# A gated linear recurrence with a multiplicative FFN: from half-sequences with a scan tree to 512-token chunks in a written order

## The chip, the cores and the metric

The kernel runs on one core of a Trainium2 chip. The metric is the device time of one launch in microseconds (us). The core has TensorE (PE; its weight loads are shown apart as PEld), VectorE (DVE), ScalarE (ACT), GpSimd (POOL) and SyncE (SP), each with its own instruction queue, worked off in order, and 16 DMA engines that all queues share. PE reads SBUF and writes PSUM.

## The reference

Inputs x, r_gate and i_gate are 4 sequences x 5824 tokens x 256 channels; the result is 23296 tokens x 256. Types are float32.

```python
a_base = sigmoid(a_param)
log_a = 8.0 * sigmoid(r_gate) * np.log(np.clip(a_base, 1e-06, 1 - 1e-06))
a_t = np.exp(log_a)
norm = np.sqrt(np.maximum(1.0 - a_t * a_t, 1e-06))
x_gated = norm * sigmoid(i_gate) * x
for t in range(S):                       # per sequence and channel, h = 0 at its start
    h = a_t[:, t] * h + x_gated[:, t]
    y[:, t] = h
out = ((y @ w1) * (y @ w2)) @ w3 @ w_out   # w1, w2: 256x1024, w3: 1024x1024, w_out: 1024x256
```

Both kernels use that the last two products are linear: w3 @ w_out is formed once on the chip as a 1024x256 weight (`wp_sb`), so the FFN has an "up" part (two products 256 -> 1024, multiplied elementwise) and a "down" part (1024 -> 256).

## The kernel before

Channels lie on partitions (two blocks of 128, `NCB`), time along the free axis. The outer loops run over 4 sequences and 2 halves of 2912 tokens (`HSEG`, `T`). A half goes through four steps.

1. Gates (lines 160-207): for each group of up to 512 tokens, POOL issues the loads of r, i and x, cast to bf16 by the DMA; PE transposes each into PSUM; ACT takes the sigmoid of r into `a_big` (L190) and of i into `sig_i` (L199); DVE multiplies `sig_i` with the transposed x into `b_big` (L206).
2. Over the whole half (L210-L214): ACT's Exp gives the decay `a_big`, Square and Sqrt give the norm in `t_big`, and DVE multiplies it into `b_big`.
3. The scan, all on DVE: a tree over blocks of 8, 4, 7 and 13 (`LEVELS`). In each block of 8, seven steps of three instructions over every eighth element (L223-L225), then `rec_scan` on the block ends (L122-L147), then the carry goes back into the blocks (L250-L255), which write `y_bf`. `hprev` hands the state from the first half to the second.
4. FFN: for each group of 512 tokens, 8 steps m of `pa` (L265) and `pb` (L270), ACT copies `pa` to `sa` (L275), DVE makes `gt` = `sa` x `pb` (L277); then 32 matmuls `pout` (L290), copied to `ot` (L299) by ACT and DVE in turn and stored over SP's queue.

Ahead of the loops, w3 is loaded whole, transposed on PE and multiplied with w_out (L85-L102). The order on each engine comes from the framework's scheduler, which orders instructions by dependence and priority, within what the buffers allow: `bigpool` and `ybuf` have two buffers each, so the gates of the next half may run beside the scan or FFN of this one. PSUM has 4 banks for `pa`/`pb`, 2 for the transposes and 2 for `pout`.

Of the kernel before, what the change touches and what calls it, by code (L numbers as in the profile page):

```python
# [10 lines left out]
AF = mybir.ActivationFunctionType  # L12


@with_exitstack
def kernel(
# [14 lines left out]

# [16 lines left out]
    NG = (T + GT - 1) // GT

    consts = ctx.enter_context(tc.tile_pool(name="consts", bufs=1))  # L50
    wpool = ctx.enter_context(tc.tile_pool(name="wpool", bufs=1))
    psum = ctx.enter_context(tc.tile_pool(name="psum", bufs=4, space=bass.MemoryType.PSUM))
    psum_t = ctx.enter_context(tc.tile_pool(name="psum_t", bufs=2, space=bass.MemoryType.PSUM))
    psum_o = ctx.enter_context(tc.tile_pool(name="psum_o", bufs=2, space=bass.MemoryType.PSUM))

    ident = consts.tile([P, P], F32, tag="ident")
    make_identity(nc, ident)
    ident_bf = consts.tile([P, P], BF16, tag="ident_bf")
    make_identity(nc, ident_bf)

    log_a8 = consts.tile([P, NCB], F32, tag="log_a8")
    nc.sync.dma_start(out=log_a8, in_=a_param.rearrange("(cb p) -> p cb", p=P))
    nc.scalar.activation(out=log_a8, in_=log_a8, func=AF.Sigmoid)
    nc.scalar.activation(out=log_a8, in_=log_a8, func=AF.Ln)
    nc.scalar.mul(out=log_a8, in_=log_a8, mul=8.0)

    w1_sb = wpool.tile([P, NCB, DFF], BF16, tag="w1")
    nc.gpsimd.dma_start(out=w1_sb, in_=moe_w1.rearrange("(cb p) f -> p cb f", p=P))
    w2_sb = wpool.tile([P, NCB, DFF], BF16, tag="w2")
    nc.gpsimd.dma_start(out=w2_sb, in_=moe_w2.rearrange("(cb p) f -> p cb f", p=P))  # L70
    wp_sb = wpool.tile([P, KD, D], BF16, tag="wp")

    with tc.tile_pool(name="wtemp", bufs=1) as wtemp:
        w3_sb = wtemp.tile([P, KD, DFF], F32, tag="w3")
        nc.sync.dma_start(out=w3_sb, in_=moe_w3.rearrange("(ko p) f -> p ko f", p=P))
        wo_sb = wtemp.tile([P, KD, D], BF16, tag="wo")
        nc.gpsimd.dma_start(out=wo_sb, in_=moe_w_out.rearrange("(ko p) f -> p ko f", p=P))

        w3T_sb = wtemp.tile([P, KD, DFF], BF16, tag="w3T")
        for jo in range(KD):  # L80
            for ii4 in range(2):
                pt = psum_t.tile([P, 4, P], F32, name="pt", tag="ptr")
                for ii in range(4):
                    i_in = ii4 * 4 + ii
                    nc.tensor.matmul(  # L85
                        out=pt[:, ii, :],
                        lhsT=w3_sb[:, i_in, jo * P:(jo + 1) * P],
                        rhs=ident, is_transpose=True,
                        start=(ii == 0), stop=(ii == 3))
                nc.scalar.copy(  # L90
                    out=w3T_sb[:, jo, ii4 * 4 * P:(ii4 * 4 + 4) * P],
                    in_=pt.rearrange("p a b -> p (a b)"))

        for mi in range(KD):
            po = psum_t.tile([P, D], F32, name="po", tag="ptr")
            for k in range(KD):
                nc.tensor.matmul(
                    out=po,
                    lhsT=w3T_sb[:, k, mi * P:(mi + 1) * P],
                    rhs=wo_sb[:, k, :],  # L100
                    start=(k == 0), stop=(k == KD - 1))
            nc.scalar.copy(out=wp_sb[:, mi, :], in_=po)  # L102

    bigpool = ctx.enter_context(tc.tile_pool(name="bigpool", bufs=2))
    ybuf = ctx.enter_context(tc.tile_pool(name="ybuf", bufs=2))
    carry = ctx.enter_context(tc.tile_pool(name="carry", bufs=2))
    inpool = ctx.enter_context(tc.tile_pool(name="inpool", bufs=1))
    tmp_pool = ctx.enter_context(tc.tile_pool(name="tmp", bufs=3))
    small = ctx.enter_context(tc.tile_pool(name="small", bufs=1))
    gpool = ctx.enter_context(tc.tile_pool(name="gpool", bufs=8))  # L110
    opool = ctx.enter_context(tc.tile_pool(name="opool", bufs=2))

    def rec_scan(a, b, levels, top=False):
# [228 lines left out]
```

## Time and profile before

| | |
|---|---|
| device time, three runs | 1126.17, 1127.95, 1128.27 us (median 1127.95) |
| profiled execution, span from first to last instruction | 1126.3 us |
| PE / PEld busy | 677.1 us (60%) / 412.9 us (37%) |
| DVE busy | 830.8 us (74%) |
| ACT busy | 553.8 us (49%) |
| POOL busy | 122.7 us (11%) |
| mean granted TensorE clock | 0.774 of full speed |
| DMA | 66.19 MB, mean 59 GB/s |

No time of the profiled execution apart from its span is recorded; the span lies within the range of the three runs, and 1.65 us under their median. Shares are means over stages of different kinds, so a stage has to be read by itself. The slices of the page divide the span into 40 equal parts of 28.2 us; a digit is the busy share in tenths. PE's ends are modelled and its matmuls overlap, so its progress is read better from the starts of successive matmuls than from its busy time.

### The profile page before, as it was taken

How to read it: one execution, taken by the hardware profiler on the slowest of the kernel's cores; microseconds unless marked ns; L12 is line 12 of the kernel's file. 1: busy time of each engine (PE TensorE's matmuls, PEld its weight loads, DVE VectorE, ACT ScalarE, POOL GpSimd, SP SyncE). 2: the span in 40 equal slices, each digit the busy share in tenths (PEclk: the TensorE clock that was granted, in tenths of full speed). 3: DMA queues.
4: the chain of work that ended last, by engine and by line, in shares of the span. 5: the costliest groups of instructions: out<-in, count | busy, mean ns of one | idle time of the engine just before them, and what ended most of it. 6: DMA issues, size and time to landing. Idle time of an engine off the chain costs nothing.

```text
span 1126.3 us, 12072 instructions
## 1 busy us (share of the span) xinstructions
PE 677.1 (60%) x4197; PEld 412.9 (37%) x4240; DVE 830.8 (74%) x1308; ACT 553.8 (49%) x733; POOL 122.7 (11%) x179
## 2 busy tenths in 40 slices
PE   2733238849952317884993332885896141689498
PEld 2522214435541213452562221443554121245155
DVE  0118999995533999998551799999663399999855
ACT  2584563424467284342558447342455828234144
POOL 2222200000021210001002221000002120000000
PEclk9755559988975558996995555998898555799699
DMA  9576521122164642113117552211316360001011
GB/s 252 76 93 75 68 29 45 38 46 62 39 107 54 77 56 38 38 39 50 57 52 102 65 69 28 55 38 42 56 48 107 45 87 0 19 33 43 13 57 51
DMA packets 100365, 66.19 MB, mean 59 GB/s; under 512 B 4560, under 2 KB 98768, under 8 KB 100304
## 3 DMA queue, kind: packets, MB, share of 16 engines
q0 software_dynamic: 74160, 37.37, 26.2%
q1 hardware_dynamic: 26144, 28.06, 7.3%
q8 instruction: 33, 0.54, 0.2%
q14 instruction: 28, 0.23, 0.1%
HBM read 78.91 MB, written 23.86 MB: 91 GB/s over the span
## 4 chain that ended last, share of the span: by engine, by line
issue 45%; DVE 23%; PE 16%; ACT 8%; DMA 4%; POOL 3%; POOLq 0%; DVEq 0%
PE pb L270 5%; PE pa L265 5%; PE pout L290 5%; DVE isc L223 4%; DVE gt L277 3%; DVE b_big L224 3%; DMA x_t<-in_x_dram 2%; DVE b_big L206 2%; DVE t_big L250 2%; ACT a_big L210 2%; DVE y_bf L252 2%; ACT t_big L213 2%; ACT t_big L212 2%; DMA r_t<-in_r_gate_dram 2%; DVE b_big L123 1%
## 5 line engine op out<-in xcount | busy, mean ns | idle before, releaser
L275 ACT CAST sa<-pa 128x512 bf16<-128x512 f32 (+1 forms) x384 | 216.4, 564 | 271.8 <-PE pa L265 107.8
L277 DVE TENSOR_TENSOR gt<-sa,pb 128x512 bf16<-128x512 bf16 (+1 forms) x384 | 248.0, 660 | 44.4 <-ACT sa L275 30.4
L265 PE MATMUL pa<-y_bf,w_sb 128*128 128x512 bf16 (+1 forms) x740 | 223.2, 380 | 82.4 <-DVE y_bf L252 58.2
L270 PE MATMUL pb<-y_bf,w_sb 128*128 128x512 bf16 (+1 forms) x753 | 226.8, 381 | 11.5 <-DVE gt L277 8.0
L290 PE MATMUL pout<-wp_sb,gt 128*128 128x256 bf16 (+1 forms) x1472 | 187.5, 273 | 5.4 <-DVE gt L277 4.0
L187 PE MATMUL pr<-ident_bf,r_t 128*128 128x128 bf16 (+1 forms) x368 | 50.2, 281 | 183.8 <-ACT sig_i L199 108.6
L290 PEld LDWEIGHTS <-gt 128*128 128x128 bf16 (+1 forms) x1472 | 139.7, 99 | 56.7 <-DVE gt L277 25.9
L206 DVE TENSOR_TENSOR b_big<-sig_i,px 128x512 f32<-128x512 bf16 (+1 forms) x96 | 62.6, 655 | 132.2 <-ACT sig_i L199 116.2
L265 PEld LDWEIGHTS <-w_sb 128*128 128x128 bf16 x768 | 76.8, 100 | 160.7 <-issue 84.2
L190 ACT ACTIVATE a_big<-pr 128x512 f32<-128x512 bf16 (+1 forms) x96 | 55.2, 575 | 157.7 <-PE pr L187 157.6
L270 PEld LDWEIGHTS <-w_sb 128*128 128x128 bf16 x768 | 77.1, 100 | 104.1 <-issue 34.3
L187 PEld LDWEIGHTS <-r_t 128*128 128x128 bf16 (+1 forms) x368 | 39.0, 128 | 195.9 <-issue 194.3
L195 PE MATMUL pi<-ident_bf,i_t 128*128 128x128 bf16 (+1 forms) x368 | 50.1, 281 | 86.5 <-DVE b_big L206 46.5
L170 POOL DMA_DIRECT2D r_t<-in_r_gate_dram x48 | 35.6, 742 | 555.8 <-PE pr L187 548.5
L203 PE MATMUL px<-ident_bf,x_t 128*128 128x128 bf16 (+1 forms) x368 | 51.1, 282 | 54.7 <-ACT sig_i L199 28.1
L214 DVE TENSOR_TENSOR b_big<-b_big,t_big 128x5824 f32<-128x5824 f32 x8 | 49.8, 6226 | 45.1 <-ACT t_big L213 45.1
L224 DVE TENSOR_TENSOR b_big<-b_big,isc 128x728 f32<-128x728 f32 x56 | 82.8, 1479 | 0.3
L225 DVE TENSOR_TENSOR a_big<-a_big 128x728 f32<-128x728 f32 x56 | 82.8, 1478 | 0.0
L223 DVE TENSOR_TENSOR isc<-a_big,b_big 128x728 f32<-128x728 f32 x56 | 82.4, 1472 | 0.0
L195 PEld LDWEIGHTS <-i_t 128*128 128x128 bf16 (+1 forms) x368 | 39.1, 129 | 100.7 <-issue 95.4
L199 ACT ACTIVATE sig_i<-pi 128x512 bf16<-128x512 bf16 (+1 forms) x96 | 55.2, 575 | 37.3 <-PE pi L195 35.4
L299 DVE COPY ot<-pout 128x512 f32<-128x512 f32 x40 | 27.6, 689 | 55.6 <-PE pout L290 55.6
(52 smaller groups left out, 652.0 us busy)
## 6 DMA issues: line engine op xcount, KB each, us to landing
out_dram<-ot SPq DMA_DIRECT2D x88, 256.0 KB, 2.1
r_t<-in_r_gate_dram POOLq DMA_DIRECT2D x40, 256.0 KB, 4.2
i_t<-in_i_gate_dram POOLq DMA_DIRECT2D x40, 256.0 KB, 5.1
x_t<-in_x_dram POOLq DMA_DIRECT2D x40, 256.0 KB, 5.4
w_sb<-in_moe_w_dram SPq DMA_DIRECT2D x1, 4096.0 KB, 18.9
w_sb<-in_moe_w_dram POOLq DMA_DIRECT2D x2, 512.0 KB, 12.9
r_t<-in_r_gate_dram POOLq DMA_DIRECT2D x8, 128.0 KB, 3.6
i_t<-in_i_gate_dram POOLq DMA_DIRECT2D x8, 128.0 KB, 3.9
```

The lines of the kernel that those rows point to most:

```text
L187: nc.tensor.matmul(out=prt[:, si * P:si * P + sw], lhsT=r_t[:sw, si, cb * P:(cb + 1) * P], rhs=ident_bf[:sw, :sw], is_transpose=True, star ...
L190: nc.scalar.activation(out=a_big[:, cb, t0:t0 + gsz], in_=prt[:, :gsz], func=AF.Sigmoid)
L195: nc.tensor.matmul(out=pit[:, si * P:si * P + sw], lhsT=i_t[:sw, si, cb * P:(cb + 1) * P], rhs=ident_bf[:sw, :sw], is_transpose=True, star ...
L206: nc.vector.tensor_mul(out=b_big[:, cb, t0:t0 + gsz], in0=sig_i[:, :gsz], in1=pxt[:, :gsz])
L223: nc.vector.tensor_mul(out=tmp, in0=av[:, :, :, t], in1=bv[:, :, :, t - 1])
L224: nc.vector.tensor_add(out=bv[:, :, :, t], in0=bv[:, :, :, t], in1=tmp)
L225: nc.vector.tensor_mul(out=av[:, :, :, t], in0=av[:, :, :, t], in1=av[:, :, :, t - 1])
L265: nc.tensor.matmul(out=pa[:, :gsz], lhsT=w1_sb[:, cb, m * P:(m + 1) * P], rhs=y_bf[:, cb, t0:t0 + gsz], start=(cb == 0), stop=(cb == NCB - 1))
L270: nc.tensor.matmul(out=pb[:, :gsz], lhsT=w2_sb[:, cb, m * P:(m + 1) * P], rhs=y_bf[:, cb, t0:t0 + gsz], start=(cb == 0), stop=(cb == NCB - 1))
L275: nc.scalar.copy(out=sa[:, :gsz], in_=pa[:, :gsz])
L277: nc.vector.tensor_mul(out=gt[:, :gsz], in0=sa[:, :gsz], in1=pb[:, :gsz])
L290: nc.tensor.matmul(out=po[:tw, j, :], lhsT=g_tiles[k][:, mt * P:mt * P + tw], rhs=wp_sb[:, k, :], start=(k == 0), stop=(k == KD - 1), skip ...
```

## The change

The kernel's body is written anew. Tokens of all four sequences form one row of 23296, cut into 46 chunks: one of 256 and 45 of 512 tokens.

- Loads are f32 on SP's queue, three buffers for each of r, i and x. Gates are taken before the transposes, with tokens on partitions (`tanh_r`, `tanh_i`): a sigmoid is written as 0.5 (1 + tanh(z/2)). POOL computes 0.5 (1 + tanh) x into `u` (two instructions). PE transposes only tanh(r/2) (`tr_r`) and `u` (`tr_u`).
- `decay`: one Exp from PSUM, with 4 log(a_base) both as scale and as bias. `square` is POOL's product of the decay with itself; `root` is ACT's Sqrt; `gated` is one DVE instruction that takes the maximum with 1e-3 and multiplies with `u` from PSUM.
- The scan tree is replaced by one DVE scan instruction per channel block and chunk (`scan`), which takes the last state of the chunk before as its start (0 at a sequence's start; a chunk over such a border has two), then a cast to bf16 (`cast`).
- FFN: two of the eight m steps share one PSUM tile of two banks (`pa`, `pb`; three such tiles), so the copies and products are 1024 elements wide. `psum_t` and `psum_o` have one buffer each.
- w3 comes in eight row blocks as bf16 over POOL's queue, and the weight product is made in eight `fold` calls, two at a time in slots 0 and 1.
- The instructions stand on each engine in the order in which the program emits them (`manual_schedule`). The loop over slots s, with four positions mp each, emits: the second store of chunk s-3, up of chunk s, folds, down of chunk s-2, the transposes, `gated`, `scan` and `cast` of chunk s+2, then what the queue of gate operations has for that position, then loads. The gate operations are dealt out in groups of up to four chunks (`group_sizes`): for each chunk tanh_r, tanh_i, decays, square, and at the group's end all its roots.

The new parts, cut to their core (what is removed is the body printed above):

```diff
+    CT = 512
+    sizes = [256] + [CT] * ((NTOK - 256) // CT)
...
+    group_sizes = [1, 1, 2, 3] + [4] * 9 + [3]
...
+    loads = ctx.enter_context(tc.tile_pool(name="loads", bufs=3))
+    gates = ctx.enter_context(tc.tile_pool(name="gates", bufs=2))
+    held = ctx.enter_context(tc.tile_pool(name="held", bufs=6))
+    ypool = ctx.enter_context(tc.tile_pool(name="ypool", bufs=2))
+    ffn = ctx.enter_context(tc.tile_pool(name="ffn", bufs=3))
+    psum = ctx.enter_context(tc.tile_pool(name="psum", bufs=3, space=bass.MemoryType.PSUM))
+    psum_t = ctx.enter_context(tc.tile_pool(name="psum_t", bufs=1, space=bass.MemoryType.PSUM))
+    psum_o = ctx.enter_context(tc.tile_pool(name="psum_o", bufs=1, space=bass.MemoryType.PSUM))
...
+    ctx.enter_context(tc.manual_schedule())
...
+    def load(c):
+        n = sizes[c] // P
+        for nm, src in (("r", rf), ("i", jf), ("x", xf)):
+            t = loads.tile([P, 4, D], F32, name=nm + "_t", tag=nm)
+            nc.sync.dma_start(
+                out=t[:, :n, :],
+                in_=src[starts[c]:starts[c] + sizes[c], :].rearrange("(n p) c -> p n c", p=P))
+            T[nm, c] = t
+    def tanh_r(c):
+        n = sizes[c] // P
+        t = gates.tile([P, 4, D], BF16, name="th_r", tag="th_r")
+        nc.scalar.activation(out=t[:, :n, :], in_=T["r", c][:, :n, :], func=AF.Tanh, scale=0.5)
+        T["thr", c] = t
+    def tanh_i(c):
+        n = sizes[c] // P
+        t = gates.tile([P, 4, D], F32, name="th_i", tag="th_i")
+        nc.scalar.activation(out=t[:, :n, :], in_=T["i", c][:, :n, :], func=AF.Tanh, scale=0.5)
+        u = held.tile([P, 4, D], BF16, name="u_t", tag="u")
+        nc.gpsimd.tensor_scalar(t[:, :n, :], t[:, :n, :], 1.0, 0.5, op0=ALU.add, op1=ALU.mult)
+        nc.gpsimd.tensor_mul(out=u[:, :n, :], in0=t[:, :n, :], in1=T["x", c][:, :n, :])
+        T["u", c] = u
+    def transposes(src, n):
+        pt = psum_t.tile([P, NCB, CT], BF16, name="ptr", tag="ptr")
+        for cb in range(NCB):
+            for j in range(n):
+                nc.tensor.matmul(
+                    out=pt[:, cb, j * P:(j + 1) * P],
+                    lhsT=src[:, j, cb * P:(cb + 1) * P], rhs=ident,
+                    is_transpose=True,
+                    start=(cb == 0 and j == 0), stop=(cb == NCB - 1 and j == n - 1))
+        return pt
+    def tr_r(c):
+        T["pr", c] = transposes(T["thr", c], sizes[c] // P)
+        T["a", c] = held.tile([P, NCB, CT], F32, name="a_t", tag="a")
+    def decay(c, cb):
+        w = sizes[c]
+        nc.scalar.activation(out=T["a", c][:, cb, :w], in_=T["pr", c][:, cb, :w], func=AF.Exp,
+                             scale=la4[:, cb:cb + 1], bias=la4[:, cb:cb + 1])
+    def square(c):
+        w = sizes[c]
+        t = held.tile([P, NCB, CT], F32, name="nrm", tag="nrm")
+        nc.gpsimd.tensor_mul(out=t[:, :, :w], in0=T["a", c][:, :, :w], in1=T["a", c][:, :, :w])
+        T["n", c] = t
+    def root(c):
+        w = sizes[c]
+        nc.scalar.activation(out=T["n", c][:, :, :w], in_=T["n", c][:, :, :w], func=AF.Sqrt,
+                             scale=-1.0, bias=1.0)
+    def tr_u(c):
+        T["pu", c] = transposes(T["u", c], sizes[c] // P)
+    def gated(c):
+        w = sizes[c]
+        nc.vector.scalar_tensor_tensor(
+            out=T["n", c][:, :, :w], in0=T["n", c][:, :, :w], scalar=1e-3,
+            in1=T["pu", c][:, :, :w], op0=ALU.max, op1=ALU.mult)
+        T["h", c] = ypool.tile([P, NCB, CT], F32, name="h_t", tag="h")
+        T["y", c] = ypool.tile([P, NCB, CT], BF16, name="y_t", tag="y", bufs=4)
+    def scan(c, cb):
+        w = sizes[c]
+        cuts = [0]
+        for b in range(1, B):
+            o = b * S - starts[c]
+            if 0 < o < w:
+                cuts.append(o)
+        cuts.append(w)
+        for lo, hi in zip(cuts[:-1], cuts[1:]):
+            if (starts[c] + lo) % S == 0:
+                init = 0.0
+            else:
+                pw = sizes[c - 1]
+                init = T["h", c - 1][:, cb, pw - 1:pw]
+            nc.vector.tensor_tensor_scan(
+                T["h", c][:, cb, lo:hi], T["a", c][:, cb, lo:hi], T["n", c][:, cb, lo:hi],
+                init, ALU.mult, ALU.add)
+    def cast(c):
+        w = sizes[c]
+        nc.vector.tensor_copy(out=T["y", c][:, :, :w], in_=T["h", c][:, :, :w])
+    def up(c, mp):
+        w = sizes[c]
+        pa = psum.tile([P, 2, CT], F32, name="pa", tag="pab")
+        for q in range(2):
+            m = 2 * mp + q
+            for cb in range(NCB):
+                nc.tensor.matmul(out=pa[:, q, :w], lhsT=w1_sb[:, cb, m * P:(m + 1) * P],
+                                 rhs=T["y", c][:, cb, :w], start=(cb == 0), stop=(cb == NCB - 1))
+        sa = ffn.tile([P, 2, CT], BF16, name="sa", tag="sa")
+        nc.scalar.copy(out=sa[:, :, :w], in_=pa[:, :, :w])
+        pb = psum.tile([P, 2, CT], F32, name="pb", tag="pab")
+        for q in range(2):
+            m = 2 * mp + q
+            for cb in range(NCB):
+                nc.tensor.matmul(out=pb[:, q, :w], lhsT=w2_sb[:, cb, m * P:(m + 1) * P],
+                                 rhs=T["y", c][:, cb, :w], start=(cb == 0), stop=(cb == NCB - 1))
+        if mp == 0:
+            T["g", c] = ffn.tile([P, KD, CT], BF16, name="g_t", tag="g")
+        nc.vector.tensor_mul(out=T["g", c][:, 2 * mp:2 * mp + 2, :w], in0=sa[:, :, :w],
+                             in1=pb[:, :, :w])
+    def down(c, j):
+        if j % 2 == 0:
+            T["po", c] = psum_o.tile([P, 2, D], F32, name="po", tag="po")
+        for k in range(KD):
+            nc.tensor.matmul(out=T["po", c][:, j % 2, :],
+                             lhsT=T["g", c][:, k, j * P:(j + 1) * P], rhs=wp_sb[:, k, :],
+                             start=(k == 0), stop=(k == KD - 1), skip_group_check=True)
+    def store(c, j2):
+        n = min(2, sizes[c] // P - 2 * j2)
+        ot = ffn.tile([P, 2, D], F32, name="ot", tag="ot")
+        if j2 == 0:
+            nc.scalar.copy(out=ot[:, :n, :], in_=T["po", c][:, :n, :])
+        else:
+            nc.vector.tensor_copy(out=ot[:, :n, :], in_=T["po", c][:, :n, :])
+        t0 = starts[c] + 2 * j2 * P
+        nc.sync.dma_start(out=out[t0:t0 + n * P, :].rearrange("(j p) c -> p j c", p=P),
+                          in_=ot[:, :n, :])
+    def fold(mi):
+        w3 = ffn.tile([P, DFF], BF16, name="w3_t", tag="w3")
+        nc.gpsimd.dma_start(out=w3, in_=moe_w3[mi * P:(mi + 1) * P, :])
+        pt = psum_t.tile([P, KD, P], BF16, name="ptw", tag="ptr")
+        for k in range(KD):
+            nc.tensor.matmul(out=pt[:, k, :], lhsT=w3[:, k * P:(k + 1) * P], rhs=ident,
+                             is_transpose=True, start=(k == 0), stop=(k == KD - 1))
+        w3t = ffn.tile([P, KD, P], BF16, name="w3t", tag="w3t", bufs=2)
+        nc.vector.tensor_copy(out=w3t, in_=pt)
+        po = psum_o.tile([P, D], F32, name="pw", tag="po")
+        for k in range(KD):
+            nc.tensor.matmul(out=po, lhsT=w3t[:, k, :], rhs=wo_sb[:, k, :],
+                             start=(k == 0), stop=(k == KD - 1))
+        nc.vector.tensor_copy(out=wp_sb[:, mi, :], in_=po)
+    LEAD = 2
+    LAG = 2
+    queue = {}
+    tanh_at = {}
+    for k, g in enumerate(groups):
+        last = g[0] - LEAD - 1
+        first = groups[k - 1][0] - LEAD if k else last
+        ops = []
+        for c in g:
+            ops.append((1.04, lambda c=c: tanh_r(c)))
+            ops.append((1.04, lambda c=c: tanh_i(c)))
+            ops.append((0.7, lambda c=c: (tr_r(c), decay(c, 0))))
+            ops.append((0.7, lambda c=c: (decay(c, 1), square(c))))
+        for c in g:
+            ops.append((1.05, lambda c=c: root(c)))
+        total = sum(d for d, _ in ops)
+        npos = 4 * (last - first + 1)
+        acc = 0.0
+        for n_op, (d, fn) in enumerate(ops):
+            pos = min(npos - 1, int(npos * (acc + d / 2) / total))
+            queue.setdefault((first + pos // 4, pos % 4), []).append(fn)
+            if n_op < 4 * len(g) and n_op % 4 == 0:
+                tanh_at[g[n_op // 4]] = 4 * first + pos
+            acc += d
+    s0 = groups[0][0] - LEAD - 1
+    nc.sync.dma_start(out=la4, in_=a_param.rearrange("(cb p) -> p cb", p=P))
+    load(0)
     nc.gpsimd.dma_start(out=w1_sb, in_=moe_w1.rearrange("(cb p) f -> p cb f", p=P))
     nc.gpsimd.dma_start(out=w2_sb, in_=moe_w2.rearrange("(cb p) f -> p cb f", p=P))
+    load(1)
+    nc.gpsimd.dma_start(out=wo_sb, in_=moe_w_out.rearrange("(ko p) f -> p ko f", p=P))
+    load(2)
+    nloaded = 3
+    nc.scalar.activation(out=la4, in_=la4, func=AF.Exp, scale=-1.0)
+    nc.scalar.activation(out=la4, in_=la4, func=AF.Ln, bias=1.0)
+    nc.vector.tensor_scalar(la4, la4, -1.0, LN_LO, op0=ALU.mult, op1=ALU.max)
+    nc.vector.tensor_scalar(la4, la4, LN_HI, 4.0, op0=ALU.min, op1=ALU.mult)
+    folds = {}
+    for mi in range(KD):
+        folds.setdefault((0, mi // 2) if mi < 4 else (1, (mi - 4) // 2), []).append(mi)
+    for s in range(s0, NCH + LAG):
+        for mp in range(4):
+            if mp == 0 and 0 <= s - LAG - 1 and sizes[s - LAG - 1] > 2 * P:
+                store(s - LAG - 1, 1)
+            if 0 <= s < NCH:
+                up(s, mp)
+            for mi in folds.get((s, mp), []):
+                fold(mi)
+            d = s - LAG
+            if 0 <= d < NCH and mp < sizes[d] // P:
+                down(d, mp)
+                if mp == 1:
+                    store(d, 0)
+            c = s + LEAD
+            if 0 <= c < NCH:
+                if mp == 0:
+                    tr_u(c)
+                    gated(c)
+                elif mp in (1, 2):
+                    scan(c, mp - 1)
+                else:
+                    cast(c)
+            for fn in queue.get((s, mp), []):
+                fn()
+            while nloaded < NCH and tanh_at[nloaded] - 6 <= 4 * s + mp:
+                load(nloaded)
+                nloaded += 1
+    store(NCH - 1, 1)
```

More of the change, by code (lines that the diff above doesn't have):

```diff
@@ L54 @@
[L54 to L64, printed above, removed]
@@ L65 @@
-    nc.scalar.mul(out=log_a8, in_=log_a8, mul=8.0)
-    w1_sb = wpool.tile([P, NCB, DFF], BF16, tag="w1")
+    NTOK = B * S
+    xf = x.rearrange("b s c -> (b s) c")
+    rf = r_gate.rearrange("b s c -> (b s) c")
+    jf = i_gate.rearrange("b s c -> (b s) c")
+    CT = 512
+    sizes = [256] + [CT] * ((NTOK - 256) // CT)
+    assert sum(sizes) == NTOK
+    NCH = len(sizes)
+    starts = [sum(sizes[:c]) for c in range(NCH)]
+    group_sizes = [1, 1, 2, 3] + [4] * 9 + [3]
+    assert sum(group_sizes) == NCH
```

257 lines of the change are left out of this document (18 added, 239 removed).

## The prediction

> **What bounds the kernel now.** I read the page's engine shares and slices first, then a table of windows, then the chain's pieces in order of time.
>
> ```profile
> span 1126.3 us, 12072 instructions
> PE 677.1 (60%) x4197; PEld 412.9 (37%) x4240; DVE 830.8 (74%) x1308; ACT 553.8 (49%) x733; POOL 122.7 (11%) x179
> PE   2733238849952317884993332885896141689498
> PEclk9755559988975558996995555998898555799699
> ```
>
> No engine is full over the span, but PE's slices alternate between 2-3 and 8-9, and the granted clock follows: 5 where PE is thin. That is a program in stages.
>
> ```profile
> 350.00:400.00 50.00, 17.56 (x121) 12.76 (x121) 43.44 (x38) 21.49 (x26) 12.68 (x18) 0.50 0.56 69
> 450.00:500.00 50.00, 42.44 (x244) 23.58 (x247) 49.48 (x94) 19.78 (x35) 0.00 (x0) 1.00 0.11 38
> 1069.15:1111.39 42.24, 42.03 (x255) 24.73 (x257) 24.78 (x37) 21.10 (x37) 0.00 (x0) 1.00 0.15 51
> ...
> 1090.27 3.65 PE pout L290 x32
> 1100.83 3.65 PE pout L290 x32
> ```
>
> Columns of a window: PE, PEld, DVE, ACT, POOL, clock, DMA share, GB/s. At 350-400 us DVE is busy 43 of 50 us on the scan, PE 18. At 1069-1111 us only FFN runs: PE 42.0 of 42.2 us at clock 1.00, DVE 24.8, ACT 21.1. One FFN group of 512 tokens then takes 1100.83 - 1090.27 = 10.56 us, so 45.5 groups' worth (23296 tokens) is 480 us. The other 646 us are the weight product and stretches in which PE waits for DVE's scan and the gates. What makes those long:
>
> ```profile
> L224 DVE TENSOR_TENSOR b_big<-b_big,isc 128x728 f32<-128x728 f32 x56 | 82.8, 1479 | 0.3
> L225 DVE TENSOR_TENSOR a_big<-a_big 128x728 f32<-128x728 f32 x56 | 82.8, 1478 | 0.0
> L223 DVE TENSOR_TENSOR isc<-a_big,b_big 128x728 f32<-128x728 f32 x56 | 82.4, 1472 | 0.0
> L206 DVE TENSOR_TENSOR b_big<-sig_i,px 128x512 f32<-128x512 bf16 (+1 forms) x96 | 62.6, 655 | 132.2 <-ACT sig_i L199 116.2
> L214 DVE TENSOR_TENSOR b_big<-b_big,t_big 128x5824 f32<-128x5824 f32 x8 | 49.8, 6226 | 45.1 <-ACT t_big L213 45.1
> ```
>
> The first three alone are 248 us of DVE, 31 us for each of the eight half-sequences, and FFN of a half cannot begin before its scan has ended.
>
> **The change, part by part.** The work goes from halves to 46 chunks (one of 256 tokens, then 512 each). Slot s holds FFN "up" of chunk s, "down" of chunk s-2, the scan of chunk s+2, and gates of a later group. So the price is a time per slot, a start before slots are full, and a tail. Prices:
>
> ```profile
> 1096.35 0.59 PE L265 MATMUL pa<-y_bf,w_sb 128*128 128x512 bf16 x2
> 1097.21 0.59 PE L265 MATMUL pa<-y_bf,w_sb 128*128 128x512 bf16 x2
> 38.78 0.39 PE L187 MATMUL pr<-ident_bf,r_t 128*128 128x128 bf16 x4
> ...
> L277 DVE TENSOR_TENSOR gt<-sa,pb 128x512 bf16<-128x512 bf16 x320 | 214.7, 688 | 40.9 <-ACT sa L275 30.4 <-PE pb L270 9.6 <-PE pa L265 0.8
> L275 ACT CAST sa<-pa 128x512 bf16<-128x512 f32 x320 | 187.4, 586 | 249.6 <-PE pa L265 95.3 <-DVE gt L277 79.0 <-remote 50.5
> L299 DVE COPY ot<-pout 128x512 f32<-128x512 f32 x40 | 27.6, 689 | 55.6 <-PE pout L290 55.6
> L299 ACT COPY ot<-pout 128x512 f32<-128x512 f32 x48 | 28.1, 586 | 76.4 <-PE pout L290 76.4
> L145 DVE TENSOR_TENSOR b_big<-b_big,tadj 128x540 f32<-128x540 f32 x8 | 9.0, 1119 | 0.2
> L240 DVE COPY H<-b_big 128x726 f32<-128x726 f32 x8 | 6.4, 806 | 0.0
> L210 ACT ACTIVATE a_big<-a_big,log_a 128x2912 f32<-128x2912 f32 x16 | 43.6, 2723 | 0.2
> L213 ACT ACTIVATE t_big<-t_big 128x5824 f32<-128x5824 f32 x8 | 40.5, 5056 | 0.1
> L213 ACT ACT_TABLE_LOAD x8 | 10.3, 1283 | 0.1
> masks.py:199 POOL TENSOR_SCALAR_AFFINE_SELECT ident<-ident 128x128 f32<-128x128 f32 x1 | 0.3, 282 | 0.0
> L326 POOL MEMSET const-float32-0.0<- 128x1 f32 x1 | 0.1, 98 | 0.2 <-issue 0.2
> ```
>
> PE, per slot: eight m steps of 0.86 us (97.21 - 96.35) are 6.9; down 3.65; 16 transposes instead of 24 (x is no longer transposed). Four take 0.39 with their latency; 16 lie between 0.9 (spacing inside the four) and 1.56; I take 1.0. Sum 11.55 us.
>
> DVE, per slot: slopes first. 688 ns for 512 elements is about 155 + 1.04 per element, so a 1024-wide product is 1.22. Four of them are 4.88, the gated input (nrm times PSUM) 1.22. The scan instruction has no row: the lower bound is an ordinary 512 product, 0.69; the upper is the strided 540-element row, 1119/540 x 512 = 1.06; the scan feeds itself, so I take the slow end: two are 2.12. The cast is 1024 elements at the 806/726 of the H copy: 1.14; bounds 0.6 (half of that) and 1.22. The ot copy is 0.69. Sum 10.05. Against it goes all of the scan tree and of the x product; DVE's total falls from 831 to about 46 x 10 = 460 us. [...]
>
> ACT, per slot: four double-width copies of 586 + 427 = 1.01 each, 4.05; two tanh and one root of 1024 elements at 5056/5824 plus the fixed part, 1.05 each, 3.15; two decays of 512 with pointer scale and bias, 0.7 each (the 2912 row has 0.3 fixed); one ot copy 0.59; two table switches of 1.28 per group of four chunks, 0.64. Sum 9.83.
>
> POOL, per slot: it takes over x_t's product (1+tanh, times x, and the square). Nothing here shows POOL arithmetic but the 128-wide select, 282 ns: at most 8 x 0.282 = 2.26 for 1024 elements; with the 0.1 of a one-element memset taken off as fixed, (0.282 - 0.1) x 8 + 0.1 = 1.55. I take 1.55 for the one-input instruction and 2.26 for each two-input one: 6.1 us, under half of a slot, so hidden; bounds 4.7 and, two-input at twice the select, 10.6. If the cover goes, ACT's tanh_i waits for th_i (two buffers) and PE's copies queue behind it on ACT.
>
> Loads leave POOL's queue for SP's, as f32 without cast:
>
> ```profile
> q1 hardware_dynamic: 26144, 28.06, 7.3%
> out_dram<-ot SPq DMA_DIRECT2D x88, 256.0 KB, 2.1
> r_t<-in_r_gate_dram POOLq DMA_DIRECT2D x40, 256.0 KB, 4.2
> L170 POOL DMA_DIRECT2D r_t<-in_r_gate_dram x48 | 35.6, 742 | 555.8 <-PE pr L187 548.5
> ```
>
> 71.6 MB of loads and 23.9 MB of stores at q1's rate (28.06 MB in 82 us of all engines) are 280 us: hidden under twice that. On SP's queue a load may wait for POOL's product of three chunks earlier; the stores behind it have three buffers, so a few us cost nothing. POOL loses its issues of 0.74 us.
>
> **The slot's loop.** The sums alone would give 11.55 (PE). But psum_o has one buffer, and the queues are in order. Count from T0, the end of DVE's ot copy for the chunk's second half, which stands first in a slot on DVE, behind the cast. Down of the next chunk may start then: 0.9, and tr_u to T0+1.5; gated runs 1.55-2.8. The second pb ends at 3.25, its product at 4.5, scan at 5.55. ACT has the ot copy (after down, 4.05) and a gate operation (to 5.8-6.1) ahead of the third sa, which ends at 6.8-7.1; product 8.1-8.4; scan 9.2-9.5. ACT's next gate operation delays the fourth sa to 8.9-9.5, its product ends at 10.7, cast 11.85, ot copy 12.55. With the cast at its low bound it is 12.0. So a slot is 12.0-12.55 and PE idles about 0.8 of it, waiting for ot; I take 12.4, with 0.1 for a tr_r that waits behind gated in the one psum_t buffer once per group (about 1.4 in four slots, mostly absorbed). From slot 2 to 45: 44 x 12.4 = 546.
>
> **Start and tail.**
>
> ```profile
> 3.03 0.20 ACT L63 ACTIVATE log_a<-log_a 128x2 f32<-128x2 f32 x1 [1.01 <-DMA log_a<-in_a_param_dram]
> 3.25 1.28 ACT L64 ACT_TABLE_LOAD   x1
> 1120.74 2.04 PE pout L290 x17
> ```
>
> The constants end at about 4.8 on ACT as now. Then one ordered chain: chunk 0 (table, tanh, decay, square on POOL, table, root) to 11; chunk 1 to 22; chunks 2 and 3 to 39, since the last root waits for POOL (two chunks of 6.1 behind the second tanh_i). The first sa of slot 0 stands behind that root. Before, PE had the folded weights at 39; now the eight folds stand in slots 0 and 1, in pairs, and their w3 loads on POOL's queue behind gate arithmetic: each batch lands 4-5 us after POOL comes to it, PE waits for it in order, tr_r behind it, the decay behind that on ACT. A fold is transposes 0.9, copy 1.22, product 0.9-1.7, about 3.5; eight are 28. Pairs come at 46, 58, 80 and 86; slot 2 starts at about 95. Bounds: 75, with the loads issued early, and 110.
>
> Tail: two slots of down alone, each 3.65 and two waits for the single psum_o of 0.85, and as now (1126.3 - 1122.8) 3.5 behind the last product: 14.
>
> Sum: 95 + 546 + 14 = 655, less about 5 for slots 43-45, which have no gates: 650 on the scale of the span of 1126.3; the runs' median of 1127.95 is 1.7 above, within this sum's rounding.
>
> **Rivals.** B, PE paces: DVE's queue never lags, the cast is short. 11.4 per slot: 95 + 502 + 14 = 611. For it: at 1069 us PE holds 99% with ACT and DVE beside it. Against: DVE now has 10 of 12 us.
>
> C, POOL and DVE hold each other up. Each of the two scans and the cast waits for the rest of a POOL instruction: half of 2.26, met half the time (6.1 of 12.4 us), 0.55 x 3 = 1.7 a slot on DVE, which sets the loop: 14.0, 616 + 109 = 725. Against it, DVE's 1.47 us products ran beside POOL's DMA issues at 350-400 us (12.68 us x18, 0.70 each, no longer than elsewhere), but those read no tile. [...] No run here shows GpSimd arithmetic beside DVE.
>
> D, tanh and exp need a table switch between them: two more of 1.28 a chunk, ACT 12.4 and in order: about 13.4 a slot, 590 + 109 = 699. For it, the rows above: eight roots, eight switches, so a change of function can cost one each time; no tanh is in the trace.
>
> E, slower than before: POOL is the bound. From (1126 - 109)/44 = 23.1 us a slot on, that is 7.7 us for each of its three instructions, 3.4 times my bound; then tanh_i waits for th_i, and all of ACT's queue with it. Only the absence of a row speaks for it.
>
> **Numbers.** Forecast (12.0-12.9 a slot, 625-680) 0.43; B 0.18; C 0.29, shading down to 680; D 0.06; E 0.03; no change 0.01. The time is 650. The range takes B without its short start, and C: 600-735. Faster by over 0.2% (what a measurement here can tell) 0.96, same 0.01, slower 0.03.
>
> **What would show it.** Right: PE busy over 85% and clock near 1.0 from about 95 us to the end, a slot of about 12.4 us, PE's longest waits on the ot copies, scans near 1.1 us. C: scans or casts that end late with POOL busy, or POOL's products well over 2.3 us. B: PE's waits below 0.3 us a slot. Wrong start: first pout far from 95. The forecast fails if POOL's busy time nears the span or ACT's table loads pass 40.

## The result and the profile after

The changed kernel takes 685.9 us (median, 684.71 to 687.18) against 1127.93 us: a ratio of 0.6084, interval [0.6074, 0.6094]. 650 was forecast, in a range of 600 to 735, so the direction and the range held and the point was 36 us low. The changed kernel's page, in its engine shares and slices:

```profile
span 685.4 us, 9681 instructions
PE 555.9 (81%) x3784; PEld 346.3 (51%) x3784; DVE 492.2 (72%) x438; ACT 440.6 (64%) x492; POOL 274.1 (40%) x155
...
PE   0326478788897898898887898898898898899995
...
PEclk9999599899999999999998999999999999999999
```

The alternation of 2-3 and 8-9 is gone. PE is thin for the first 100 us (six slices of 17 us) and then stands at 7-9: from 96.4 to 671.7 us it is busy 88% at a granted clock of 0.99. In the last slices, where gates and POOL are through, it stands at 9. DVE's total fell from 831 to 492 us (460 was worked out) and no engine is full, so what remains is a start and a wait in each slot. The pieces of the forecast can be read off the timeline, line by line of kernel.py; here PE and DVE of slots 2 and 46-47:

```profile
96.40 1.02 PE L178 MATMUL pa<-y_t,w_sb 128*128 128x512 bf16 x4 [0.23 <-DVE g_t L190]
99.28 1.04 PE L197 MATMUL po<-wp_sb,g_t 128*128 128x256 bf16 x8
...
671.66 1.91 PE L197 MATMUL po<-wp_sb,g_t 128*128 128x256 bf16 x16 [1.22 <-DVE ot L207]
681.51 0.69 DVE L207 COPY ot<-po 128x512 f32<-128x512 f32 x1 [4.63 <-PE po L197]
```

Slot 2 begins at 96.4 us (95 forecast), the two slots of down alone begin at 671.7, and the tail is 685.4 - 671.7 = 13.7 (14 forecast). Between them lie 44 slots in 575.3 us: 13.07 each, where 12.4 was forecast. The miss is there. One group of four slots, by the starts of `gated` (L144) on DVE at 305.40, 318.59, 330.92, 345.90 and 357.28, takes 13.2, 12.3, 15.0 and 11.4 us, and the same four repeat to 0.05 us through the kernel. The exceptions are the first groups, the end, and two of the three places where a chunk holds a sequence's border (15.2 and 16.2 us, and 13.7 and 13.9 in the slot behind). Two stretches of DVE's timeline, and POOL's in the first of them, show what differs:

```profile
339.05 1.99 DVE L164 TENSOR_TENSOR_SCAN h_t<-a_t,h_t,nrm 128x512 f32<-128x512 f32 x1
340.96 1.19 DVE L190 TENSOR_TENSOR g_t<-sa,pb 128x1024 bf16<-128x1024 bf16 x1
342.07 1.66 DVE L170 CAST y_t<-h_t 128x1024 bf16<-128x1024 f32 x1
343.65 0.68 DVE L207 COPY ot<-po 128x512 f32<-128x512 f32 x1
...
338.92 1.05 POOL L104 TENSOR_SCALAR th_i<-th_i 128x1024 f32<-128x1024 f32 x1 [2.67 <-PE pa L178]
340.05 3.13 POOL L105 TENSOR_TENSOR u_t<-th_i,x_t 128x1024 bf16<-128x1024 f32 x1
...
344.38 1.03 PE L197 MATMUL po<-wp_sb,g_t 128*128 128x256 bf16 x8 [1.61 <-DVE ot L207]
...
352.12 1.28 DVE L164 TENSOR_TENSOR_SCAN h_t<-a_t,h_t,nrm 128x512 f32<-128x512 f32 x1
354.42 0.69 DVE L170 CAST y_t<-h_t 128x1024 bf16<-128x1024 f32 x1
```

The same scan takes 1.28 us with POOL idle and 1.99 beside POOL's tensor_scalar, the same cast 0.69 and 1.66. POOL's product is stretched as well, to 3.13 from the 2.34 that it takes at other places. Behind the late cast stands the ot copy, and behind that PE: it waits 1.61 us for it. From the list of waits of the changed kernel:

```profile
DVE g_t L190 <- ACT sa L181: 100.9, 101, 10.9
...
PE po L197 <- DVE ot L207: 51.5, 39, 3.5
```

### The profile page after: what moved, and what is told of

Its sections match the earlier page's. It is cut to its first block, busy times and chain, and to the rows that moved or that the text cites. A ratio compares the mean times of both kernels' runs of the same rounds, so it can differ in the third digit from the quotient of the medians.

```text
span 685.4 us, 9681 instructions
## 1 busy us (share of the span) xinstructions
PE 555.9 (81%) x3784; PEld 346.3 (51%) x3784; DVE 492.2 (72%) x438; ACT 440.6 (64%) x492; POOL 274.1 (40%) x155
## 4 chain that ended last, share of the span: by engine, by line
PE 35%; DVE 23%; issue 18%; ACT 14%; DMA 6%; POOL 3%; SPq 1%; DVEq 0%; ACTq 0%; POOLq 0%
PE po L197 14%; PE pa L178 8%; DVE g_t L190 7%; PE pb L186 7%; ACT sa L181 7%; DVE h_t L164 5%; DMA i_t<-in_i_gate_dram 5%; DVE y_t L170 4%; DVE ot L207 4%; PE ptr L112 4%; PE pw L223 2%; ACT a_t L125 2%; DVE nrm L144 2%; ACT th_i L102 2%; POOL nrm L131 1%
## 5 line engine op out<-in xcount | busy, mean ns | idle before, releaser
L190 DVE TENSOR_TENSOR g_t<-sa,pb 128x1024 bf16<-128x1024 bf16 (+1 forms) x184 | 220.9, 1200 | 111.5 <-ACT sa L181 100.9
L181 ACT CAST sa<-pa 128x1024 bf16<-128x1024 f32 (+1 forms) x184 | 184.2, 1001 | 118.6 <-PE pa L178 116.5
L197 PE MATMUL po<-wp_sb,g_t 128*128 128x256 bf16 x1456 | 189.3, 274 | 53.2 <-DVE ot L207 51.5
L197 PEld LDWEIGHTS <-g_t 128*128 128x128 bf16 x1456 | 142.7, 98 | 115.2 <-issue 66.1
L186 PE MATMUL pb<-y_t,w_sb 128*128 128x512 bf16 (+1 forms) x736 | 190.3, 382 | 2.9 <-ACT sa L181 2.9
L178 PE MATMUL pa<-y_t,w_sb 128*128 128x512 bf16 (+1 forms) x736 | 191.6, 384 | 0.2 <-DVE g_t L190 0.2
L164 DVE TENSOR_TENSOR_SCAN h_t<-a_t,h_t,nrm 128x512 f32<-128x512 f32 (+3 forms) x90 | 137.2, 1526 | 0.0
L131 POOL TENSOR_TENSOR nrm<-a_t 128x1024 f32<-128x1024 f32 (+1 forms) x46 | 99.1, 2153 | 79.8 <-ACT a_t L125 79.8
L105 POOL TENSOR_TENSOR u_t<-th_i,x_t 128x1024 bf16<-128x1024 f32 (+1 forms) x46 | 117.8, 2562 | 5.9 <-DMA x_t<-in_x_dram 2.1
L125 ACT ACTIVATE a_t<-ptr,la 128x512 f32<-128x512 bf16 (+1 forms) x92 | 66.7, 772 | 68.4 <-PE ptr L112 68.4
L144 DVE SCALAR_TENSOR_TENSOR nrm<-nrm,ptr 128x1024 f32<-128x1024 f32 (+1 forms) x46 | 55.6, 1209 | 38.2 <-PE ptr L112 20.3
L102 ACT ACTIVATE th_i<-i_t 128x1024 f32<-128x1024 f32 (+1 forms) x46 | 48.4, 1052 | 2.5 <-DMA i_t<-in_i_gate_dram 2.5
L112 PE MATMUL ptr<-ident,u_t 128*128 128x128 bf16 x364 | 30.6, 232 | 11.1 <-POOL u_t L105 10.2
## 6 DMA issues: line engine op xcount, KB each, us to landing
wo_sb<-in_moe_w_out_dram POOLq DMA_DIRECT2D x1, 512.0 KB, 14.3
```

What stands on the lines that cost most here:

```text
L105: nc.gpsimd.tensor_mul(out=u[:, :n, :], in0=t[:, :n, :], in1=T["x", c][:, :n, :])
L112: nc.tensor.matmul(out=pt[:, cb, j * P:(j + 1) * P], lhsT=src[:, j, cb * P:(cb + 1) * P], rhs=ident, is_transpose=True, start=(cb == 0 and ...
L125: nc.scalar.activation(out=T["a", c][:, cb, :w], in_=T["pr", c][:, cb, :w], func=AF.Exp, scale=la4[:, cb:cb + 1], bias=la4[:, cb:cb + 1])
L131: nc.gpsimd.tensor_mul(out=t[:, :, :w], in0=T["a", c][:, :, :w], in1=T["a", c][:, :, :w])
L144: nc.vector.scalar_tensor_tensor(out=T["n", c][:, :, :w], in0=T["n", c][:, :, :w], scalar=1e-3, in1=T["pu", c][:, :, :w], op0=ALU.max, op1 ...
L164: nc.vector.tensor_tensor_scan(T["h", c][:, cb, lo:hi], T["a", c][:, cb, lo:hi], T["n", c][:, cb, lo:hi], init, ALU.mult, ALU.add)
```

## The experiments

The theory: a slot of 12.0-12.5 us comes from the ordered queues and the one psum_o buffer, and on top of it some instructions of DVE and POOL collide: beside each other they take longer, as the scan (1.28 and 1.99 us) and the cast (0.69 and 1.66) above. Rivals: gates come late through POOL (a dependence, not a collision), or DVE's own work paces. In the table, "first down" is the start of the first `po` product on PE, "rest" is the span less that, so that start and slots can be told apart. Both are of the profiled execution, whose time lies up to 4 us off the median.

| kernel | median us | ratio to before | first down | rest |
|---|---|---|---|---|
| changed kernel | 685.9 | 0.6084 [0.6074, 0.6094] | 99.3 | 586.1 |
| no POOL arithmetic (e1) | 620.9 | 0.5499 [0.5487, 0.5510] | 78.6 | 541.1 |
| POOL arithmetic, unread (e2) | 684.2 | 0.6062 [0.6048, 0.6076] | 96.5 | 586.5 |
| POOL only writes (e9) | 630.2 | 0.5589 [0.5565, 0.5613] | 85.2 | 545.0 |
| tr_r moved (e4) | 681.9 | 0.6038 [0.6025, 0.6050] | 99.7 | 580.6 |
| store early (e3) | 644.7 | 0.5717 [0.5696, 0.5737] | 97.7 | 545.3 |
| no cast (e6) | 640.5 | 0.5681 [0.5666, 0.5697] | 95.9 | 542.3 |
| no cast, u on DVE (e8) | 638.1 | 0.5656 [0.5642, 0.5671] | 94.2 | 542.0 |
| w3 at once (e5) | 675.2 | 0.5987 [0.5963, 0.6012] | 92.2 | 581.9 |
| w3 at slot -1 (e10) | 668.5 | 0.5922 [0.5910, 0.5933] | 82.4 | 582.0 |
| all, POOL kept (e11) | 621.4 | 0.5504 [0.5483, 0.5526] | 81.3 | 534.3 |
| all, u on DVE (e12) | 612.2 | 0.5421 [0.5408, 0.5435] | 79.3 | 528.1 |
| all, no POOL (e13) | 650.0 | 0.5752 [0.5734, 0.5770] | 93.5 | 555.4 |

**Collision or dependence.** Three kernels: without POOL's arithmetic; with it, but unread; with POOL writing only. All three leave the product with x and the square of the decay out of the result.

```diff
 e1: tanh_i, square, root
-        nc.gpsimd.tensor_scalar(t[...], t[...], 1.0, 0.5, op0=ALU.add, op1=ALU.mult)
-        nc.gpsimd.tensor_mul(out=u[...], in0=t[...], in1=T["x", c][...])
+        (ACT's Tanh writes u)
-        nc.gpsimd.tensor_mul(out=t[...], in0=T["a", c][...], in1=T["a", c][...])
+        (the root reads T["a", c])
 e2: as e1, and beside it
+        nc.gpsimd.tensor_scalar(t[...], u[...], 1.0, 0.5, op0=ALU.add, op1=ALU.mult)
+        nc.gpsimd.tensor_mul(out=v[...], in0=t[...], in1=T["x", c][...])
+        nc.gpsimd.tensor_mul(out=sq[...], in0=T["a", c][...], in1=T["a", c][...])
 e9: as e1, and in tanh_i
+        for _ in range(5):
+            nc.gpsimd.memset(T["x", c][:, :n, :], 0.0)
```

> POOL does no arithmetic: tanh of i goes straight from ACT into u as bf16 (the product with x and the 1+ are left out), and the root takes the decay itself (the square is left out). Loads, ACT's, PE's and DVE's instructions keep their number and size. Collision theory (a scan or cast of DVE and a POOL instruction cannot run at once): every scan 1.28 us, every cast 0.69 us, slots of 11.1-11.8 us where now four slots take 13.2, 12.3, 15.0 and 11.4; with a shorter start (no root waits for POOL, w3 loads early in POOL's queue, slot 2 at about 76 us) 76 + 44 x 11.6 + 14 = 600 us. Queue theory of the prediction (the single psum_o buffer and the in-order queues alone give 12.0-12.55 a slot): slots stay at 12 or more, 76 + 540 + 14 = 630 us.

> As the kernel without POOL arithmetic, but POOL does its three instructions per chunk of the same size beside it, into tiles that nobody reads. Collision theory: scans and casts are stretched as before (means 1.5 and 1.1 us), four slots take 50-52 us, total about 665-680 us (only the start is shorter, by waits of roots for POOL). Rival, dependence theory (slots are long because gates reach PE and DVE late through POOL): slots of 11.1-11.8 us as without POOL arithmetic, 600-615 us.

> As the kernel without POOL arithmetic, but POOL writes zeros over each chunk's x tile five times, about 4.7 us a chunk, without reading SBUF. Theory P (any POOL instruction on SBUF holds up a scan or cast): scans and casts stretch as with unread arithmetic, 665-684 us. Theory R (a scan meets only POOL instructions that read): scans 1.28 us, casts stretched at times, 621-632 us.

Unread arithmetic costs the whole of it: 684.2 us against 620.9, slot by slot as in the changed kernel. So gates that come late through POOL are not the cause; POOL's presence is. The groups of the scan and the cast, first without POOL arithmetic, then with it unread, then with POOL's memsets (mean ns of one behind the comma):

```profile
L160 DVE TENSOR_TENSOR_SCAN h_t<-a_t,h_t,nrm 128x512 f32<-128x512 f32 x84 | 107.2, 1278 | 0.0
L166 DVE CAST y_t<-h_t 128x1024 bf16<-128x1024 f32 x45 | 30.9, 686 | 0.0
```

```profile
L166 DVE TENSOR_TENSOR_SCAN h_t<-a_t,h_t,nrm 128x512 f32<-128x512 f32 x84 | 131.1, 1562 | 0.0
L172 DVE CAST y_t<-h_t 128x1024 bf16<-128x1024 f32 x45 | 51.6, 1148 | 0.0
```

```profile
L162 DVE TENSOR_TENSOR_SCAN h_t<-a_t,h_t,nrm 128x512 f32<-128x512 f32 x84 | 107.2, 1277 | 0.0
L168 DVE CAST y_t<-h_t 128x1024 bf16<-128x1024 f32 x45 | 35.5, 788 | 0.0
...
L104 POOL MEMSET x_t<- 128x1024 f32 x225 | 217.6, 969 | 283.5 <-DMA x_t<-in_x_dram 273.2
```

POOL's instructions that read and write stretch both, by 2 x 0.28 + 0.46 = 1.03 us a slot; POOL's 218 us of writing alone leave the scan at 1.28 and touch the cast seldom: 8 of the 45 of 1024 elements take 0.75 to 1.47 us, the others 0.68-0.69. Theory R of the third expectation held, though the memsets do not stand at the same moments as the arithmetic. In the rest, e2 and e1 differ by 45.4 us, 1.03 us a slot. That the two figures are equal is chance: the repeated group of four differs by 52.1 - 48.5 us, 0.91 a slot, and the remainder stands mostly at the two borders; nor does each us of stretch lengthen a slot by one, as the store's place will show.

Without POOL the slots did not fall to 11.1-11.8 on the whole: the four of a group take 12.0, 11.8, 13.7 and 11.0, in the mean 12.1, and 620.9 us lies between the two expectations. The queue theory's 12.0-12.5 is thus what remains without collisions, but in the mean only, from single slots of 11.0 to 13.7.

**The slot of 15 us.** The third chunk's tr_r is put one position later, away from tr_u.

```diff
+            if len(g) == 4 and n_op in (10, 11) and pos % 4 == 0:
+                pos += 1
```

> Only the place of one gate operation per group of four changes: the third chunk's tr_r, decays and square go from the position that also holds tr_u and gated to the next one. Theory that the 15.0 us slot is long because tr_r waits there for gated in the one psum_t buffer, and ACT's decay and the next sa behind it: that slot falls to about 13.3, 1.6 us in each of some 10 groups, 670 us. Rival, that its excess is all collisions of scan and cast with POOL: within 5 us of 686.

Only 0.6 us of that slot went (15.0 to 14.4), 4 us in all. That total is the rival's case, but its reason is not the rival's alone: e1 has the slot at 13.7 without any collision, so about 1.3 of its excess is collision. Part of what tr_r gave up went into the wait for the ot copy: PE waits 2.38 us for it at the end of that slot, where it waited 1.61. With the cast gone, the same move is worth 0.9 (13.7 in e6, 12.8 in e11, whose other changes lie in the start or leave the order on DVE as it is). What holds the rest isn't settled.

**The queue behind psum_o.** The store's copy goes ahead of the cast on DVE; or the cast goes.

```diff
 e3:
-            if mp == 0 and 0 <= s - LAG - 1 and sizes[s - LAG - 1] > 2 * P:
-                store(s - LAG - 1, 1)
...
+                if mp == 3:
+                    store(d, 1)
...
-    store(NCH - 1, 1)
 e6: scan
-                init = T["h", c - 1][:, cb, pw - 1:pw]
+                init = T["y", c - 1][:, cb, pw - 1:pw]
...
-                T["h", c][:, cb, lo:hi], T["a", c][:, cb, lo:hi], T["n", c][:, cb, lo:hi],
+                T["y", c][:, cb, lo:hi], T["a", c][:, cb, lo:hi], T["n", c][:, cb, lo:hi],
 e6: cast
-        nc.vector.tensor_copy(out=T["y", c][:, :, :w], in_=T["h", c][:, :, :w])
+        pass
```

> Only the place of the second store of a chunk changes: right behind the chunk's last down, ahead of the cast, instead of at the head of the next slot. Queue theory (the one psum_o buffer makes down wait for an ot copy that stands behind a stretched cast on DVE): PE's waits for DVE's ot copy fall from 51 us to under 15, some 0.5-0.8 us a slot, total 650-665. Rival (DVE is full with collisions, so the wait only moves to the cast and to gated): within 8 us of 686.

> The scan writes the bf16 tile itself and takes its start from it, so the cast instruction is gone (a chunk's starting state is rounded to bf16). DVE loses 1.12 us a slot with its collisions. Collision theory: a scan still stretches, 1.5 us in the mean; the slots with a stretched cast (13.2, 12.3, 15.0) each lose 0.5-1.2, the slot of 11.4 loses nothing since PE paces it: 655-665 us in all. Rival (PE and ACT pace all slots, the cast was cover): 680 or more.

One moved line is worth 41 us: 644.7. The scans still take 1552 ns in the mean, yet the rest is 545, nearly as short as with no POOL arithmetic at all (541); the slots are 12.3, 11.2, 13.9 and 10.4. PE's wait for DVE's ot copy falls from 51.5 to 15.3 us. The cast, which now stands later, also meets POOL less: 789 ns in the mean instead of 1138. The two rows of this run, from its waits and its groups:

```profile
PE po L197 <- DVE ot L207: 15.3, 14, 2.5
...
L170 DVE CAST y_t<-h_t 128x1024 bf16<-128x1024 f32 x45 | 35.5, 789 | 0.0
```

So most of what the stretched scan and cast cost came by way of the ot copy, which stood behind them with PE's down behind it, in the one psum_o buffer. What the scans' stretch still costs in the new order isn't shown: no kernel has the early store without POOL arithmetic. Taking the cast away does the same to the queue (rest 542, PE's wait 14.9 us). Both gains were larger than expected, and neither rival fits.

**Less work on POOL.** On top of the kernel without the cast, u is made by one DVE instruction.

```diff
-        nc.gpsimd.tensor_scalar(t[...], t[...], 1.0, 0.5, op0=ALU.add, op1=ALU.mult)
-        nc.gpsimd.tensor_mul(out=u[...], in0=t[...], in1=T["x", c][...])
+        nc.vector.scalar_tensor_tensor(out=u[...], in0=t[...], scalar=1.0,
+                                       in1=T["x", c][...], op0=ALU.add, op1=ALU.mult)
...
-  Sqrt, scale=-1.0, bias=1.0         scalar=1e-3 in gated
+  Sqrt, scale=-0.25, bias=quarter    scalar=5e-4 in gated
```

> As the kernel without the cast, and (1 + tanh) x is one DVE instruction of 1024 elements from SBUF (the half is folded into the root's scale and bias); POOL keeps the square alone, 1.9 us a chunk. DVE without collisions: 4.9 + 1.2 + 1.2 + 2.6 + 0.7 = 10.6 us a slot. Collision theory: fewer and shorter collisions, slots of 12.0-12.6 us, start shorter by the roots' waits for POOL: 85 + 44 x 12.3 + 14 = 640 us. Rival, that DVE's own work is what counts: 1.2 us more on DVE costs at least as much as the collisions gave, 660-690 us.

638.1 us, 2.4 less than without it, which is less than the spread of either kernel's runs (3.3 and 3.7 us): the rest is 542 both times. The total is as expected, the slots are not better: the scans fell to 1319 ns, 0.46 us a slot, against 1.2 us more work on DVE, and the repeated group went from 47.7 to 48.4 us while the slots at the borders got shorter. What each of the two is worth by itself isn't separated here.

**The start.** The w3 loads are issued by POOL at once, or in a gap at slot -1; in both, `fold` finds them in eight buffers.

```diff
+    for mi in range(KD):
+        T["w3", mi] = ffn.tile([P, DFF], BF16, name="w3_t", tag="w3", bufs=KD)
+        nc.gpsimd.dma_start(out=T["w3", mi], in_=moe_w3[mi * P:(mi + 1) * P, :])
 e5: ahead of the loop over s;  e10: in it, at s == -1 and mp == 0
```

> All eight w3 loads are issued by POOL ahead of the slot loop, into eight buffers. Start theory of the prediction (folds wait for loads that stand on POOL's queue behind gate arithmetic): slot 2 begins at 68-76 us instead of 96, total 658-666 us, slots unchanged. Rival, that ACT's chain of tables and gates sets the start anyway: slot 2 at 90 or later, 680 us or more; the early w3 loads may also delay the first r and i loads by 2-4 us.

> Only the w3 loads move: all eight are issued at the head of slot -1, in a gap of POOL's queue (24-28 us), behind the loads of the first chunks, into eight buffers. With the early issue at 5 us the first gates came 7.7 us later and the start still shortened by 7; if folds wait for POOL's queue and those 7.7 us were the first loads' contention, slot 2's first down now starts at 84-86 us instead of 99 and the total is 669-674 us. Rival (ACT's chain sets the start): first down at 90 or later, 677 us or more.

At once, the gain is 10.7 us, between the two cases of the expectation, since the first `gated` comes at 22.5 us instead of 14.9. The delay is POOL's queue: its last three w3 issues wait for loads that it issued earlier, and POOL's first gate instruction stands behind them, at 18.87 us instead of 9.19, though ACT ended that tanh at 8.0.

```profile
18.32 0.53 POOL L263 DMA_DIRECT2D w_t<-in_moe_w_dram  x1 [5.46 <-DMA wo_sb<-in_moe_w_out_dram]
18.87 0.63 POOL L104 TENSOR_SCALAR th_i<-th_i 128x512 f32<-128x512 f32 x1
```

The second expectation put those 7.7 us down to the loads' contention, which is thus not the nearest cause. At slot -1 the first down starts at 82.4 and the total is 668.5, as expected and a little better. The rest keeps its 582.

**All together.** Store early, no cast, w3 at slot -1 and tr_r moved, with three ways of making u and the square.

```diff
 e13, on top of e12: square
-        nc.gpsimd.tensor_mul(out=t[:, :, :w], in0=T["a", c][:, :, :w], in1=T["a", c][:, :, :w])
+        nc.scalar.activation(out=t[:, :, :w], in_=T["a", c][:, :, :w], func=AF.Square)
```

> No cast, second store behind its down, w3 loads at slot -1, third tr_r of a group moved; POOL keeps its three instructions. Collision theory: scans still stretched to 1.5 us in the mean; the gains of the cast and of the store overlap (both take the ot copy from behind the cast), so 640 less 14 for w3 and 4 for tr_r: 618-626 us.

> The same with (1 + tanh) x on DVE and the square alone on POOL: 638 less 14 and 4, 615-624 us. Scans near 1.3 us. If DVE's 10.6 us a slot now pace, no better than the kernel with POOL's three instructions.

> The same with the square on ACT as well, so POOL does no arithmetic and nothing collides: scans all 1.28 us. ACT has 10.9 us a slot, DVE 10.6, PE 11. Collision theory: slots of 11.3-11.8 us, 75 + 44 x 11.5 + 14 = 595 us. Rival (ACT's ordered queue becomes the pace, 1.06 us a slot more): 12 or more a slot, 615-630 us.

The best is e12, 612.2 us, 74 below the changed kernel and below e1, which leaves the work out. Making u on DVE is worth 9 us here (e11 to e12). In e12's repeated slots PE is busy 97% (428.6 of 440 us from 120 us on) and a slot takes 11.7 us, close to the prediction's PE sum of 11.55. Freeing DVE of all collisions by giving ACT the square is 38 us slower than that; it went the rival's way, and 20 us beyond its range. The page's shares and the longest waits of e13:

```profile
PE 549.9 (85%) x3784; PEld 343.0 (53%) x3784; DVE 467.3 (72%) x439; ACT 486.5 (75%) x538; POOL 7.4 (1%) x17
...
DVE g_t L193 <- ACT sa L184: 119.5, 105, 4.8
```

and of e12:

```profile
PE 539.3 (89%) x3784; PEld 340.4 (56%) x3784; DVE 471.4 (78%) x439; ACT 441.8 (73%) x492; POOL 100.7 (17%) x63
...
DVE g_t L193 <- ACT sa L184: 84.2, 103, 3.4
```

ACT is busy 75% of e13's span and 83% of its repeated slots (371.9 of 450 us from 135 us on), and with 1.06 us more on it a slot grew by 0.8 us, 11.7 to 12.5, though DVE's scans lost their stretch: DVE's wait for `sa` grew from 84 to 120 us. An engine that works in order can delay others well below full. But ACT's work is not all of the 38 us. POOL, with no arithmetic to hold it up, issues the w3 loads at 4.0 us in e13, where e12 has them at 23.4:

```profile
4.02 2.70 POOL L282 DMA_DIRECT2D w_t<-in_moe_w_dram  x5
...
23.44 4.33 POOL L282 DMA_DIRECT2D w_t<-in_moe_w_dram  x8
```

As in e5, the start is late then (first `pa` at 37.8 us against 31.4, first down at 93.5 against 79.3). The rest grew by 27 us; how the 14 us of the start divide between the loads and ACT isn't separated.

## Why the prediction was right, and where it was off

- **Start and tail** held: slot 2 at 96.4 against 95, tail 13.7 against 14. The mechanism did too. ACT's chain ended its roots at 14.8, 25.4 and 40.9 us, where 11, 22 and 39 were counted. The four pairs of folds were put at 46, 58, 80 and 86 us; their transposes begin at 44.7, 54.3, 75.9 and 86.8, with PE waiting for loads behind gate arithmetic on POOL, and e10 takes 17 us of it away.
- **The queue's loop**, 12.0-12.55 without collisions, is what e1 shows in the mean (12.1), and e3 shows its link: the copy behind the cast, worth 41 us. The prediction named the link and took it as given. The close number is partly luck: single slots run from 11.0 to 13.7, which the count does not have, and PE waits for the ot copy 14.3 us in all in e1, 0.3 us a slot, where about 0.8 was counted.
- **The step that failed is the sum's choice of no cost for POOL beside DVE** (12.4 with 0.1 for everything else). It measures 1.03 us a slot (e2 less e1), 45 us, and that is more than the 36 us that the point was low, mainly since a slot without it takes 12.1 and not 12.4. The time lies outside the forecast's own 625-680, and the slot of 13.07 outside its 12.0-12.9: the stated range held because it took in rival C. Of the signs, PE's 88% and its longest waits on the ot copies were the forecast's; scans of 1.54 us in the mean and POOL products of up to 3.13 were C's. Rival C had the meeting of the two; its 1.7 a slot, and so 725 us, were too much, and its path, DVE setting the loop, is not the one that e3 shows, in which the delay goes through the ot copy to PE. It took the meeting of the two as chance, but in an emitted order the same instructions meet each time: in each group one scan meets a reading instruction for 1.3 us, one for 0.7, and one slot of four meets none. The truth lies between the forecast (0.43) and C (0.29).
- **Prices.** Products 1.21, `sa` 1.01, tanh 1.06, gated 1.22 and ot 0.68 came out to 0.02; the decay is 0.78 instead of 0.7. The scan alone is 1.28, not 1.06, and the cast alone 0.69, not 1.14; the two errors cancel to 0.01 a slot. POOL's tensor_scalar is 1.04 undisturbed instead of 1.55, its products 1.9 and 2.34 around the 2.26 taken.
- **The cast's price** was that of the H copy, whose elements lie apart: 806 ns for 726, 1.11 ns an element. In e1 the cast of 1024, which lie together, takes 686 ns, 0.67 an element; what makes the difference isn't shown. The slots were not shorter for it, since the longer scan and the collisions filled the place.
- **Rivals B, D and E.** B's 11.4 a slot is seen where POOL and the gates are quiet (11.1 from 619 us on, with PE busy 51.2 of 52.7 us, and no tr_r among its work), so PE could hold about that. D fell: tables are loaded 14 times each for tanh and Sqrt in the trace, one pair a group, and none between tanh and exp. E was far: POOL is busy 40%.

```profile
L96 ACT ACT_TABLE_LOAD x14 | 18.0, 1283 | 0.3
L136 ACT ACT_TABLE_LOAD x14 | 18.0, 1283 | 0.3
```

## What to carry to other kernels

In a pipeline with a written order, look at what stands ahead of the instruction that frees a single buffer: putting a 0.7 us copy ahead of a cast was worth 41 us, nearly as much as taking the cast away (45). Price work moved to POOL by what it does to the instructions that DVE runs beside it, not by whether POOL has time; here scans went from 1278 to 1562 ns in the mean and casts from 686 to 1148 (e1, e2), and 40% POOL cost 1 us of each 13 us slot. And an engine that is busy 83% of a slot can lengthen it when others wait for it in order, so a relief for one engine (DVE in e13) is to be set against the waits that it makes on the other. Last, an issue that has to wait holds what stands behind it in an ordered queue: with the w3 loads sent out at once (e5), the first down comes 10 us later than with the same loads at slot -1 (e10).

## What the runs showed of the hardware

- A scan from two SBUF tiles and an SBUF to SBUF cast on DVE take 1.28 and 0.69 us alone (e1) and up to 3.33 and 1.67 beside POOL arithmetic (changed kernel); there `g_t`, with one operand in PSUM, keeps 1.19-1.22 beside it. POOL's product is stretched too, 2.34 to 3.13. Beside memsets on POOL the scan keeps its time (1277 ns, e9), while the cast grows at times (788 ns in the mean against 686). What sets the stretched ones apart isn't shown: DVE's `u` in e8 reads two SBUF tiles as well, and twice (at 33.1 and 88.7 us), with POOL's square beside it for 1.11 and 0.75 us, it took 1.19 and 1.20, against 1.21 in the mean.
- The scan takes 2.06 ns an element, from 1278 and 1146 ns at 512 and 448 elements in e1. A product takes 1.03 there, from 1217 and 688 ns of `g_t` at 1024 and 512 elements, half of the scan's.

```profile
L160 DVE TENSOR_TENSOR_SCAN h_t<-a_t,h_t,nrm 128x448 f32<-128x448 f32 x2 | 2.3, 1146 | 0.0
```
